# Summing the query-state product of odd chunks in the banks of the score-value product

## The chip, the cores and the metric

One core of one Trainium2 chip runs the whole kernel. The metric is the device time of one execution in microseconds (us), the median of the runs shown.

## The reference

A delta-rule recurrence (four sequences, 8 heads, 768 steps, head size 48), and then a feed-forward layer on its output (3072 tokens, 384 in, 768 hidden).

```python
for t in range(S):
    kt, vt, bt = (k_n[:, :, t], v[:, :, t], beta[:, :, t, None])
    y[:, :, t] = np.einsum('bhd,bhde->bhe', q[:, :, t], state)
    v_old = np.einsum('bhde,bhd->bhe', state, kt)
    state = state + bt[:, :, :, None] * np.einsum('bhd,bhe->bhde', kt, vt - v_old)
...
h = np.maximum(np.maximum(x @ w1, x @ w2), x @ w3)
return (h @ w_out).astype(np.float32)
```

`k_n` is k divided by its norm. x is y with the heads of a token put side by side.

## The kernel before, in words

**Chunks.** The 768 steps are cut into 12 chunks of 64 (`C`). Within a chunk the recurrence is turned into matrix products; only the state `st` (48 x 48 for each sequence and head) goes from chunk to chunk. Two chunks form a group; there are 6 groups (`GROUPS`). The feed-forward layer works on 512 tokens, those of a group, at a time.

**The products of a chunk c.** A chunk has 8 heads and 4 sequences, so 32 small products of each kind, and the array of 128 x 128 is used as four quarters of 64 x 64: the quarter is given by which half of the partitions the operands lie on (row half) and which half the result goes to.
- `old_k` (letter k, lines 750 to 757): keys times state, in `times_state` (line 736, tile p_k, matmuls L743); VectorE subtracts it from the values (L755).
- `old_q` (letter q, lines 759 to 763): queries times state, also in `times_state` (p_q, L743); ScalarE copies it to the tile qs (L763), of which there is one buffer.
- `new` (letter u, L771): the block's triangular inverse times what `old_k` left (p_u); ScalarE copies it to u (L776).
- `step` (letter s, L794): keys times u (p_s); VectorE adds it to the state (L801).
- `to_y` (letter y, L813): masked scores times u (p_y); VectorE adds qs to it (L815), which gives the chunk's y.
- `to_x` (letter x, L832 to L841) turns y into the layer's x on TensorE; from group 2 on `y_blocks`, `read_y` and `turn_y` (letters x, w, X) do it by two transfers and a VectorE transpose (L872).

The inverse comes from a substitution on VectorE (`solve`, L561 and L565) and from products that join its halves (e, f, z and j: `halves_z`, `halves_u` with L696 and its copies L700, `join_z` L713, `join_u` L726). t or T is `turn` (L338, the transposes of keys and queries), g or P is `gram` (L415, scores), M masks scores (L399), and S is one step of `solve`.

**PSUM.** The eight banks are two for the layer (tag "ffn") and three pairs (tag "two", `ps_two`, line 92), one bank for each half of a chunk's sequences. All the products of the recurrence use the pairs. A pair is taken when a product starts and comes free when its reader is done; the pair that has been free longest is taken next. `solve(1)` (group 1) keeps its running sum y_p in a pair from line 524 until its last step (L569).

**Order.** The schedule is written by hand; each engine works in program order. The layer of group m is a generator, `ffn(m)`, whose units (three matmuls of p_h, L1224, or six or more of p_o) are yielded one by one, and after each unit the entries for that step are issued. `FIRST` holds, by step of `ffn(0)`, the recurrence of chunk 1 and the queries that are turned; `EARLY_LINKS` holds group 1 (chunks 2 and 3) in the later steps of `ffn(0)`; `LINKS`, `FOURTH_LINKS` and `LAST_LINKS` hold the later groups. In a name such as "k1", the digit says which chunk of the group. After T4 to T7 `queries` issues the load of a later query block (`load_q`, SyncE's queue). In `ffn(0)` a step also converts a piece of the layer's weights (`weights`: ScalarE L247 to L249, VectorE L259, GpSimd L263).

Of the kernel before, what the change touches and what calls it, by code (L numbers as in the profile page):

```python
# [23 lines left out]
def kernel(  # L24
# [31 lines left out]
    nc = tc.nc  # L56

    B, H, S, D = q.shape
# [5 lines left out]
    NP = H // 2  # L64
# [27 lines left out]
    def ps_two(name):  # L92
        return pairs.tile([128, 2, 512], FP32, name=name, tag="two", bufs=3)
# [24 lines left out]
    def rows(bb):  # L118
        return slice(C * bb, C * (bb + 1))

    def dims(par):
        return slice(DP * par, DP * par + D)
# [77 lines left out]
    st = const.tile([128, 2, 2, NP, D], FP32, name="st")  # L200
# [113 lines left out]
    kqts, ats, pts, xs, at_d = {}, {}, {}, {}, {}  # L314
# [89 lines left out]
    def gram(n, parts=(0, 1), queues=one_queue, copy=nc.scalar.copy, later=False):  # L404
        kqt, g = kqts[n], n % 2
        p_g = ps_two("p_g")

        whole = len(parts) == 2 and not g
        for j in range(NP):
            for par in range(2):  # L410
                for bb in range(2):
                    kq = kqt[dims(par), j, bb ^ g]
                    for i in (0,) if whole else parts:
                        c0 = j * 128 + i * C
                        nc.tensor.matmul(  # L415
                            p_g[
                                rows(bb ^ (g * i)), par, c0 : c0 + C * (1 + whole)
                            ],
                            kq[:, 0],
                            kq if whole else kq[:, i],  # L420
                        )
        p_v = p_g.rearrange("p two (j i t) -> p two j i t", j=NP, i=2)
        if 1 in parts:
            pt = pts[n] = square("pt")
            if later:
                copy(by_par(pt), p_v[:, :, :, 1])
            else:
                masked(pt, p_v[:, :, :, 1])
        if 0 not in parts:
            return  # L430
        at = ats[n] = square("at")
        copy(by_par(at), p_v[:, :, :, 0])  # L432
        if queues:
            to_dram(n, queues)
# [181 lines left out]
    def both(name, w, bufs=1):  # L616
        return work.tile([128, 2, H, w], FP32, name=name, bufs=bufs)

    def by_head(t, w):
        return t[:, :, 0 : H * w].rearrange("p g (h x) -> p g h x", x=w)  # L620
# [3 lines left out]
    def block(bb, f=0, n=BL):  # L624
        return slice(C * bb + BL * f, C * bb + BL * f + n)
# [23 lines left out]
    def heads_of(c, name, w):  # L649


        copies = (nc.scalar.copy,) if c else (nc.scalar.copy, nc.vector.tensor_copy)
        n = H // len(copies)
        for i, copy in enumerate(copies):
            p_v = ps_two(name)[:, :, 0 : n * w]
            yield (
                range(i * n, i * n + n),
                p_v.rearrange("p g (h x) -> p g h x", x=w), copy,
            )
# [13 lines left out]
    def span(hs):  # L673
        return slice(hs[0], hs[-1] + 1)
# [53 lines left out]
                negate[bb](u12[block(bb), :, span(hs)], p_v[bb][block(bb)], -1.0)  # L728


    xts, rhss, qss, us, yts = {}, {}, {}, {}, {}

    def heads(t):
        return t.rearrange("p g (j two) d -> p two (g j) d", two=2)

    def times_state(kqt, i, name):
        p_b = ps_two(name)
        for j in range(NP):
            for g in range(2):
                for par in range(2):  # L740
                    for bb in range(2):
                        c0 = (g * NP + j) * D
                        nc.tensor.matmul(  # L743
                            p_b[rows(bb), par, c0 : c0 + D],
                            kqt[g][dims(par), j, bb ^ g, i],
                            st[dims(par), bb ^ g, g, j],
                        )
        return p_b[:, :, 0 : H * D].rearrange("p two (x d) -> p two x d", d=D)

    def old_k(c):  # L750
        rhss[c] = vts.pop(c)
        if c:
            kqt = [kqts[2 * c + g] for g in range(2)]
            rhs = heads(rhss[c])
            nc.vector.tensor_tensor(  # L755
                out=rhs, in0=rhs, in1=times_state(kqt, 0, "p_k"), op=ALU.subtract
            )

    def old_q(c):
        kqt = [kqts[2 * c + g] for g in range(2)]  # L760
        if c:
            qs = qss[c] = both("qs", D)
            nc.scalar.copy(heads(qs), times_state(kqt, 1, "p_q"))  # L763

    def new(c):
        rhs = rhss.pop(c)
        u = us[c] = both("u", D, 2)
        for hs, p_v, copy in heads_of(c, "p_u", D):
            for i, h in enumerate(hs):
                for bb, g in TILES:  # L770
                    nc.tensor.matmul(  # L771
                        p_v[rows(bb ^ g), g, i],
                        ut[c % NU][rows(bb), g, h],
                        rhs[rows(bb), g, h],
                    )
            copy(u[:, :, span(hs)], p_v)  # L776
        if c + NU < 2 * FINE:
            for bb in range(2):
                corner = ut[c % NU][block(bb), :, :, BL:C]
                zero = kpad[0][block(bb), None, 0:1, D : D + 1]  # L780
                nc.scalar.copy(corner, zero.to_broadcast(corner.shape))
# [23 lines left out]
    def to_y(c):  # L805
        u = us[c]
        pt = [pts.pop(2 * c + g) for g in range(2)]
        y = yts[c] = both("y", D)
        for hs, p_v, copy in heads_of(c, "p_y", D):
            for i, h in enumerate(hs):  # L810
                for bb, g in TILES:
                    r = rows(bb ^ g)
                    nc.tensor.matmul(p_v[rows(bb), g, i], pt[g][r, h], u[r, g, h])  # L813
            if c:
                nc.vector.tensor_tensor(out=y, in0=qss.pop(c), in1=p_v, op=ALU.add)  # L815
            else:
                copy(y[:, :, span(hs)], p_v)
# [536 lines left out]
    for _ in range(2):  # L1354
# [6 lines left out]
    join_u(0)  # L1361
    masked(pts[1], by_par(pts[1]))
    old_k(0)
    old_q(0)
    new(0)
    some(conv, 1)
    fetch(nc.gpsimd)
    load_v(1, nc.gpsimd)
    placed(1, 3)
    to_y(0)  # L1370
    halves_t(1)
    solving = solve(1)
# [6 lines left out]

    LINKS = {  # L1380
# [3 lines left out]
    }  # L1384
    FOURTH_LINKS = {
# [2 lines left out]
    }  # L1388
    LAST_LINKS = {
        0: "k0 q0", 6: "p1", 8: "d0 d1 z0 z1", 9: "j0 j1", 10: "u0", 11: "s0 y0",  # L1390
        12: "x0 k1 q1", 13: "u1 w0", 14: "y1 x1", 15: "w1", 16: "X0", 19: "X1",
    }

    STEPS = {
# [6 lines left out]
    EARLY_LINKS = {  # L1401
# [3 lines left out]
    }  # L1405


    FIRST = {
# [3 lines left out]
    }  # L1412


    RECURS = dict(
        z=join_z, j=join_u, k=old_k, q=old_q, u=new, s=step, y=to_y, x=to_x,
        e=halves_z, f=halves_u, d=turn_t1,
    )
    MADE = dict(V=load_v, P=prep_values)
# [2 lines left out]
        g=lambda n: gram(n, queues=(nc.gpsimd,) * 2 if n in (10, 11) else one_queue),  # L1422
# [132 lines left out]
```

## Time and profile before

| | |
|---|---|
| median of the 3 runs shown | 505.97 us (505.88 to 508.54) |
| span of the profiled execution, first to last instruction | 505.2 us |
| TensorE matmul busy, share of the span | 484.0 us, 96% |
| VectorE busy | 361.1 us, 71% |
| ScalarE busy | 169.4 us, 34% |
| GpSimd busy | 187.1 us, 37% |
| mean granted TensorE clock | 0.968 |

The profiled execution's own time outside the span is not listed; its span lies 0.8 us below the median of the runs. PE is TensorE's matmuls, PEld its weight loads, DVE VectorE, ACT ScalarE, POOL GpSimd, SP SyncE. A matmul of this kernel's 32-bit numbers leaves two records, so 32 matmuls read "x64". An arrow `a<-b` in a tile column reads "a, made from b"; `<-DVE v_t L755` after an idle time names what ended it.

### The profile page before, as it was taken

To read this page: it belongs to the slowest core of one execution; us is meant where nothing else is said; L and a number is where in the kernel's file an instruction comes from. 1 tells how busy PE (TensorE), PEld (TensorE's weight loads), DVE (VectorE), ACT (ScalarE), POOL (GpSimd) and SP (SyncE) were. 2 spreads that over 40 slices of the span, in tenths; PEclk is the share of its full clock that TensorE was granted. 3 is DMA by queue.
4 is the path that set the end of the run, shared out by engine and by line. 5 is a ranking of instruction groups with operands and counts; after the bars stand their busy time and mean duration, and the time that the engine had idled before them with its cause. 6 is when DMAs were issued, how large, how long until landed. Compare 5 with 4: busy or idle time off the path is not lost.

```text
span 505.2 us, 18676 instructions
## 1 busy us (share of the span) xinstructions
PE 484.0 (96%) x8064; PEld 338.0 (67%) x8064; DVE 361.1 (71%) x835; ACT 169.4 (34%) x320; POOL 187.1 (37%) x311
## 2 busy tenths in 40 slices
PE   7678989999999999999999999999999999999996
PEld 6467767855566555565565565555797457998895
DVE  5888799787996441799652999565998874468753
ACT  5585664885422142210152200242201032212210
POOL 7434472793391935770395880501000020000000
PEclk9855899999999999999999999999999999999999
DMA  8937869864045934544584652744224230340002
GB/s 114 205 50 214 195 142 160 198 181 137 3 120 134 191 72 77 146 119 117 112 156 104 158 137 74 149 72 96 64 54 90 47 86 15 85 94 1 0 18 47
DMA packets 109121, 53.50 MB, mean 106 GB/s; under 512 B 92208, under 2 KB 102864, under 8 KB 109040
## 3 DMA queue, kind: packets, MB, share of 16 engines
q1 hardware_dynamic: 97280, 31.78, 31.0%
q0 software_dynamic: 9216, 19.85, 16.5%
q8 instruction: 63, 1.03, 0.9%
q10 hardware_dynamic: 2544, 0.69, 0.8%
q14 instruction: 18, 0.15, 0.1%
HBM read 39.17 MB, written 13.11 MB: 103 GB/s over the span
## 4 chain that ended last, share of the span: by engine, by line
PE 76%; DVE 11%; ACT 4%; DMA 3%; SPq 3%; issue 2%; POOL 0%; DVEq 0%; ACTq 0%; POOLq 0%
PE p_h L1224 28%; PE p_o L985 13%; PE p_o L1262 12%; PE p_c L1163 5%; DVE tmp L561 3%; PE p_g L415 2%; PE p_m L905 2%; PE p_u L771 2%; PE p_k L743 2%; DVE y_p L565 2%; DMA kmore<-in_k_dram 2%; PE p_y L813 2%; PE p_s L794 2%; PE p_q L743 1%; PE p_j L726 1%
## 5 line engine op out<-in xcount | busy, mean ns | idle before, releaser
L1224 PE MATMUL p_h<-xt,w_sb 128*128 128x512 f32 (+1 forms) x450 | 186.8, 558 | 0.6 <-ACT xt L839 0.6
L1224 PEld LDWEIGHTS p_h<-xt,w_sb 128*128 128x128 f32 x450 | 82.4, 193 | 69.2 <-issue 61.6
L1238 DVE TENSOR_TENSOR h<-h,p_h 128x512 f32<-128x512 f32 (+1 forms) x42 | 25.5, 607 | 46.8 <-PE p_h L1224 46.3
L565 DVE TENSOR_TENSOR y_bl<-y_bl,tmp 128x31 f32<-128x31 f32 (+20 forms) x139 | 50.4, 363 | 4.8
L561 DVE TENSOR_TENSOR tmp<-x_bl,y_bl 128x31 f32<-128x31 f32 (+20 forms) x139 | 48.8, 351 | 3.9
L1262 PE MATMUL p_o<-wo_sb,h 128*128 128x384 f32 x144 | 48.9, 490 | 0.0
L373 POOL DMA_DIRECT2D turned<-in_q_dram x72 | 39.3, 554 | 4.6 <-POOL turned L368 3.1
L1262 PEld LDWEIGHTS p_o<-wo_sb,h 128*128 128x128 f32 x144 | 26.7, 190 | 17.2
L1234 ACT ACTIVATE h<-p_h 128x512 f32<-128x512 f32 x24 | 14.3, 597 | 69.2 <-PE p_h L1224 69.2
L263 POOL TENSOR_TENSOR w_sb<-mant,up 128x384 int32<-128x384 int32 x18 | 19.0, 1054 | 39.5 <-DVE mant L259 37.8
L415 PEld LDWEIGHTS p_g<-kqt 48*64 48x64 f32 x1216 | 24.5, 142 | 9.2 <-issue 6.3
L415 PE MATMUL p_g<-kqt 48*64 48x64 f32 (+1 forms) x1216 | 27.7, 241 | 0.9 <-ACT kqt L344 0.8
L1268 ACT COPY o_sb<-p_o 128x384 f32<-128x384 f32 x12 | 5.8, 479 | 62.6 <-PE p_o L1262 56.5
L801 DVE TENSOR_TENSOR st<-st,p_s 48x768 f32<-48x768 f32 (+1 forms) x18 | 17.1, 949 | 12.7 <-PE p_s L794 12.4
L399 DVE TENSOR_TENSOR pt<-p_g,mask 128x512 f32<-128x512 f32 x20 | 13.8, 690 | 17.0 <-PE p_g L415 16.9
L598 POOL DMA_DIRECT2D ut<-y_d x4 | 2.6, 653 | 60.6 <-DMA y_d<-y_bl 60.6
L148 POOL DMA_DIRECT2D v_t<-in_v_dram x14 | 11.6, 832 | 35.3 <-PE p_u L771 35.3
L368 POOL MEMSET turned<- 128x96 f32 x18 | 3.3, 191 | 49.4 <-DVE kqt L389 49.4
L771 PEld LDWEIGHTS p_u<-v_t,ut 64*64 64x64 f32 x768 | 13.5, 141 | 8.4 <-issue 7.3
L432 ACT COPY at<-p_g 128x512 f32<-128x512 f32 x22 | 12.8, 585 | 17.4 <-DVE pt L399 15.4
L373 POOL DMA_DIRECT2D turned<-in_k_dram x32 | 17.5, 556 | 1.2 <-POOL turned L368 1.2
L1163 PE MATMUL p_c<-xt,w_sb 128*128 128x256 f32 x72 | 17.7, 379 | 0.0
(239 smaller groups left out, 907.3 us busy)
## 6 DMA issues: line engine op xcount, KB each, us to landing
w_bits<-in_moe_w_dram SPq DMA_DIRECT2D x9, 384.0 KB, 6.2
w_bits<-in_moe_w_dram POOLq DMA_DIRECT2D x9, 384.0 KB, 5.7
turned<-in_q_dram POOLq DMA_DIRECT2D x72, 48.0 KB, 2.8
out_dram<-o_sb SPq DMA_DIRECT2D x36, 96.0 KB, 2.3
y_x<-y SPq DMA_DIRECT2D x32, 96.0 KB, 3.0
qall<-y_x SPq DMA_DIRECT2D x32, 96.0 KB, 2.8
v_t<-in_v_dram POOLq DMA_DIRECT2D x14, 192.0 KB, 5.0
at_d<-at SPq DMA_DIRECT2D x72, 32.0 KB, 3.0
```

Source lines behind the costliest of these rows:

```text
L263: nc.gpsimd.tensor_tensor(out=dst.bitcast(I32), in0=mant_v.bitcast(I32), in1=up_v, op=ALU.add)
L373: (queue, nc.gpsimd)[i].dma_start(out=t[p0 : p0 + 32, bb, at : at + NP * 2 * D].rearrange("p (j x) -> p j x", j=NP), in_=(k, q)[i][2 * bb ...
L415: nc.tensor.matmul(p_g[rows(bb ^ (g * i)), par, c0 : c0 + C * (1 + whole)], kq[:, 0], kq if whole else kq[:, i],)
L561: nc.vector.tensor_tensor(out=t_v, in0=row.to_broadcast(t_v.shape), in1=column.to_broadcast(t_v.shape), op=ALU.mult,)
L565: nc.vector.tensor_tensor(out=rest, in0=rest, in1=t_v, op=ALU.subtract)
L771: nc.tensor.matmul(p_v[rows(bb ^ g), g, i], ut[c % NU][rows(bb), g, h], rhs[rows(bb), g, h],)
L801: nc.vector.tensor_tensor(out=s_v[r], in0=s_v[r], in1=p_s[r, :, 0 : H * D], op=ALU.add)
L985: nc.tensor.matmul(to[:, g], a[j][:, 128 * g : 128 * (g + 1)], b[j], start=(start and g == j == 0), stop=(stop and g == 1 and j == len(a) ...
L1163: nc.tensor.matmul(to, w[stays], moves, start=(n == 0), stop=(n == len(terms) - 1))
L1224: nc.tensor.matmul(p_h, w_sb[i][:, t, f * 128 : (f + 1) * 128], xt[:, t, lo : lo + w], start=(t == 0), stop=(t == KT - 1),)
L1238: nc.vector.tensor_tensor(out=h, in0=h, in1=p_h, op=ALU.max)
L1262: nc.tensor.matmul(p_o, stays, moves, start=(n == 0), stop=(n == len(terms) - 1))
```

## The change

For odd chunks the query-state product is no longer written to a pair of its own and copied to qs. `old_q` now has two parts of 16 matmuls. Part 0 (letter a) takes the pair p_y and writes half of the heads into it; part 1 writes the other half into the same pair, from inside `new`, after the first half of its heads. In each part a row half of the array writes one bank. Later `to_y` adds the score-value product onto it in PSUM (`start` off), and ScalarE copies the sum to y. The pair is held from part 0 to that copy. Even chunks keep qs and the addition (`even_q`); the call for chunk 0, which did nothing but look up tiles, is gone. In the tables, q of odd chunks is gone, "a1" stands ahead of "k1", and x0 of group 1 moves one step, behind s1.

```diff
-    def old_q(c):
+    def old_q(c, part):
+        if part == 0:
+            sums_y[c] = by_head(ps_two("p_y"), D)
+        for j in range(NP):
+            for g in range(2):
+                par = g ^ part
+                for bb in range(2):
+                    nc.tensor.matmul(
+                        sums_y[c][rows(bb), g, 2 * j + par],
+                        kqts[2 * c + g][dims(par), j, bb ^ g, 1],
+                        st[dims(par), bb ^ g, g, j],
+                        start=(part == 0 and j == 0),
+                        stop=False,
+                    )
+    def even_q(c):
         kqt = [kqts[2 * c + g] for g in range(2)]
-        if c:
-            qs = qss[c] = both("qs", D)
-            nc.scalar.copy(heads(qs), times_state(kqt, 1, "p_q"))
+        qs = qss[c] = both("qs", D)
+        nc.scalar.copy(heads(qs), times_state(kqt, 1, "p_q"))
 
     def new(c):
...
             for i, h in enumerate(hs):
+                if c in sums_y and h == NP:
+                    old_q(c, 1)
                 for bb, g in TILES:
...
     def to_y(c):
...
-        for hs, p_v, copy in heads_of(c, "p_y", D):
+        if c in sums_y:
+            held = [(range(H), sums_y.pop(c), nc.scalar.copy)]
+        else:
+            held = heads_of(c, "p_y", D)
+        for hs, p_v, copy in held:
             for i, h in enumerate(hs):
                 for bb, g in TILES:
                     r = rows(bb ^ g)
-                    nc.tensor.matmul(p_v[rows(bb), g, i], pt[g][r, h], u[r, g, h])
-            if c:
+                    nc.tensor.matmul(
+                        p_v[rows(bb), g, i], pt[g][r, h], u[r, g, h],
+                        start=not c % 2, stop=(not c % 2 or h == H - 1),
+                    )
+            if c in qss:
                 nc.vector.tensor_tensor(out=y, in0=qss.pop(c), in1=p_v, op=ALU.add)
             else:
                 copy(y[:, :, span(hs)], p_v)
...
-    old_q(0)
...
     LINKS = {
...
-        5: "g2 g3 p1", 6: "u0 N0", 7: "V1 N1", 8: "s0 y0 N2", 9: "x0", 10: "k1 q1",
+        5: "g2 g3 p1", 6: "u0 N0", 7: "V1 N1", 8: "s0 y0 N2", 9: "x0", 10: "a1 k1",
...
     LAST_LINKS = {
-        12: "x0 k1 q1", 13: "u1 w0", 14: "y1 x1", 15: "w1", 16: "X0", 19: "X1",
+        12: "x0 a1 k1", 13: "u1 w0", 14: "y1 x1", 15: "w1", 16: "X0", 19: "X1",
...
     EARLY_LINKS = {
-        23: "k1 y0 q1", 24: "u1 x0", 25: "s1", 26: "y1", 28: "x1",
+        23: "a1 k1 y0", 24: "u1", 25: "s1 x0", 26: "y1", 28: "x1",
...
     FIRST = {
-        0: "e1 s0 S1 S1", 1: "f1 k1 S1 S1 S1", 2: "z1 d1 M2 S1 S1",
-        3: "j1 S1 q1 M3 S1 S1", 4: "u1 T4", 5: "y1", 6: "s1 T5", 7: "x1 T6",
+        0: "e1 s0 S1 S1", 1: "f1 a1 k1 S1 S1 S1", 2: "z1 d1 M2 S1 S1",
+        3: "j1 S1 M3 S1 S1", 4: "u1 T4", 5: "y1", 6: "s1 T5", 7: "x1 T6",
...
     RECURS = dict(
-        z=join_z, j=join_u, k=old_k, q=old_q, u=new, s=step, y=to_y, x=to_x,
+        z=join_z, j=join_u, k=old_k, q=even_q, u=new,
+        a=lambda c: old_q(c, 0), s=step, y=to_y, x=to_x,
```

More of the change, by code (lines that the diff above doesn't have):

```diff
@@ L728, in join_u @@
                 negate[bb](u12[block(bb), :, span(hs)], p_v[bb][block(bb)], -1.0)
-    xts, rhss, qss, us, yts = {}, {}, {}, {}, {}
+    xts, rhss, qss, us, yts, sums_y = {}, {}, {}, {}, {}, {}
     def heads(t):
```

## The prediction

> **What bounds the kernel now.** I read the page first (busy shares, slices), then busy time by stage, the waits of TensorE, the chain of waits in order of time, and the timeline of 40 to 136 us.
>
> ```profile
> PE 484.0 (96%) x8064; PEld 338.0 (67%) x8064; DVE 361.1 (71%) x835; ACT 169.4 (34%) x320; POOL 187.1 (37%) x311
> PE   7678989999999999999999999999999999999996
> DVE  5888799787996441799652999565998874468753
> PEclk9855899999999999999999999999999999999999
> ```
>
> TensorE is full from the eighth slice on at full granted clock; VectorE is near full only in the first quarter. By stage (span, then busy time of PE, PEld, DVE, ACT, POOL, the clock, the DMA share, GB/s):
>
> ```profile
> 54.60:81.00 26.40, 24.03 (x664) 19.93 (x658) 23.93 (x59) 17.25 (x34) 13.45 (x17) 1.00 0.84 170
> 81.00:102.00 21.00, 19.98 (x336) 16.49 (x334) 16.93 (x39) 15.59 (x29) 10.97 (x13) 1.00 0.89 176
> 102.00:130.70 28.70, 28.55 (x700) 16.05 (x691) 24.69 (x53) 16.85 (x32) 16.38 (x22) 1.00 0.48 137
> 130.70:242.70 112.00, 112.00 (x1551) 67.08 (x1552) 76.65 (x174) 28.87 (x52) 62.32 (x113) 1.00 0.49 110
> ```
>
> From 130.7 us TensorE has no idle time at all: there, VectorE or ScalarE work that is saved is worth nothing, and only matmul time counts. Chunks 1 and 3 lie before that line or on it, chunks 5, 7, 9 and 11 behind it. TensorE's waits between 44.9 and 131 us, the places where a delay can be swallowed (total, times, longest):
>
> ```profile
> PE p_t L338 <- DMA qall<-in_q_dram: 1.0, 1, 1.0
> PE p_x L832 <- DVE st L801: 0.7, 1, 0.7
> PE p_j L726 <- DVE t L632: 0.3, 1, 0.3
> ```
>
> **The odd chunks behind 130.7 us.** The chain of waits around chunk 9 (start, length, what):
>
> ```profile
> 356.81 1.08 PE p_k L743 x64
> 357.89 0.93 PE p_q L743 x64
> 358.83 2.77 PE p_h L1224 x6
> 361.60 1.08 PE p_u L771 x64
> ```
>
> Each product is 32 matmuls (64 records). One that follows another 64-row product takes 0.93, so 29 ns a matmul; the first after a 128-row matmul takes 0.15 more. The new query product is again 32 matmuls: 16 ahead of p_k and 16 inside p_u. Before: 1.08 + 0.93 + 1.08 = 3.09 us; after: a1 and k1 1.08 + 0.47, p_u 1.08 + 0.47, together 3.10. No change, but for the seams in p_u, where the last quarter of the array that p_u used is the first that the product needs. Bounds: nothing (the chain shows p_k, p_y and p_q at 0.93 each when back to back at 124.7) and, for two seams, two whole matmuls of 0.22 (the mean of p_q's row), 0.44. I take 0.05, near the row of unlike products back to back: 0.25 for chunks 3 to 11.
>
> Do new waits arise here? p_u needs VectorE's subtraction (L755). After the change only the layer's 2.77 us lie between p_k's end and p_u, not 0.93 more. At chunk 9 p_k then ends at 358.36, the subtraction runs as before from 359.07 to 360.02, and p_u starts at 361.1: 1.1 us to spare. At chunk 7 the subtraction ends at 288.07 against 288.5: tight, still free. The three bank pairs go to whoever asks in the order in which they came free; s1 gets the pair that L755 emptied long ago and doesn't wait for the copy of p_y.
>
> ```profile
> L743 PE MATMUL p_q<-st,kqt 48*64 48x48 f32 x672 | 12.2, 218 | 0.0
> L815 DVE TENSOR_TENSOR y<-qs,p_y 128x768 f32<-128x768 f32 x11 | 10.5, 952 | 4.6 <-PE p_y L813 4.4
> L763 ACT COPY qs<-p_q 128x768 f32<-128x768 f32 x11 | 8.8, 800 | 18.1 <-PE p_q L743 11.7 <-DVE y L815 4.7 <-DVE y_p L565 1.7
> ```
>
> Six L815 additions of 0.95 go from VectorE; six L763 copies go and six copies of p_y, same form, 0.80, come: ScalarE's work is unchanged. At chunks 5 to 11 the freed VectorE time is idle time. Cover gone, each would cost its 0.80.
>
> **Chunk 1: one bank pair left.** The second block solve keeps its running sum y_p in one of the three "two" pairs until 89 us. The change holds p_y of chunk 1 in a second pair from step 1 to step 5. So k1, z1, j1, u1 and T4 pass through one pair, each waiting until the one before is read out.
>
> ```profile
> 54.90 1.55 ACT L700 ACTIVATE ut<-p_f 16x256 f32<-16x256 f32 x4 [2.55 <-PE p_f L696]
> 55.91 0.95 DVE L755 TENSOR_TENSOR v_t<-v_t,p_k 128x768 f32<-128x768 f32 x1 [1.61 <-PE p_k L743]
> 66.17 0.80 ACT L776 COPY u<-p_u 128x768 f32<-128x768 f32 x1 [0.63 <-PE p_u L771]
> 70.44 0.95 DVE L815 TENSOR_TENSOR y<-qs,p_y 128x768 f32<-128x768 f32 x1
> ```
>
> Step by step, by these durations:
> - f1 ends at 54.6, a1's 16 matmuls at 55.2. k1 now needs the pair that f1's four copies (L700) read until 56.45: a wait of 1.3. k1 ends at 57.45 (before: 55.8); unit 2, queued behind, and L755, for which VectorE sits idle, slip with it: L755 by 1.64.
> - z1 (needs L755's end, 58.5) starts after unit 2 at 58.95: no more. j1 already waits for VectorE's transposes, which stand behind L755 and slip by the same 1.64. So j1 ends at 62.8 for 61.16.
> - q1's 1.08 behind j1 is gone: unit 4 is late by 0.56. u1 has 0.47 more: 1.04. T4 must wait until L776 has read p_u: 0.1 + 0.80 + 0.05, so unit 5 and y1 are late by 2.0. That is the peak.
> - y1's copy runs on ScalarE at 71.1 to 71.9. Behind it waits conversion 5 (L247 to L249, at 68.92 before), late by 3; POOL needs it only for step 11's weights, six units on.
> - Regained: the L815 at 70.44 is gone, so VectorE, without a gap from 56 to 84 us, is late by 1.64 - 0.95 = 0.69. Before, x1 waited 0.7 for L801 to empty its pair (the second row of the waits); L801 now ends at 74.94, ahead of x1's turn at 75.5. TensorE leaves x1 late by 1.2.
> - T5 and T6 start late, and SyncE issues the query loads behind them late. The load that p_t awaited at 85.84 was issued 10 us earlier, and the next one, 1.8 us younger, landed at 86.2: at a DMA share of 0.84 the backlog, not the issue, sets the landing. I let it land 0 to 1.2 late; so TensorE's lateness there becomes 0.2 to 1.2. The low end is nearer to the two landings.
> - But VectorE ends the solve 0.69 late; stores, reloads and p_z of chunk 3 (from 105.5, its data landing at 105.43) follow. So 0.5 is the floor. I take 0.6.
>
> **Chunk 3** sits on the border:
>
> ```profile
> 130.66 1.02 PEld L771 LDWEIGHTS p_u<-v_t,ut 64*64 64x64 f32 x64 [0.98 <-DVE v_t L755]
> ```
>
> p_u waits for L755, the last of a VectorE queue that is full from 115.7 and is started by ScalarE and TensorE, so it slips by the same 0.6. All 32 matmuls of q1 stood ahead of this wait; now 16 stand in p_u behind it: +0.47, in full, since everything after is solid TensorE. ScalarE's 4.7 us wait in L763 (qs has one buffer, still read by chunk 2's L815) vanishes; TensorE has no wait for ScalarE there: 0.
>
> **Sum:** 0.6 + 0.47 + 0.25 = +1.3 us on the span of 505.2. The median of the three runs shown, 505.97, is 0.8 above that span; launch and end lie around it and don't change. 505.97 + 1.3 = 507.3. The parts' ends give +0.5 + 0.47 = +1.0 and 1.2 + 0.47 + 5 x 0.44 = +3.9.
>
> **Rivals.**
> - *The lateness of chunk 1 stays whole.* If x1 does not regain 0.8 and the query load slips with its issue, 2.0 + 0.47 + 0.25 = +2.7: 508.7. For it: the wait on the single pair is in the code, and DMA is busy. Against it: TensorE had 1.7 us of waits in just these places. It decides once the load of 85.84 lands more than a microsecond later.
> - *The VectorE side gains.* Chunk 3's p_u waits 0.98 because VectorE is behind; two of its operations before that were stretched by POOL's conversions (0.90 for 0.22 at 120.63, 1.06 for 0.28 at 125.77). If the shifted order avoids these 1.4 us, the 0.98 and the 0.47 are paid from it: 0.6 + 0.25 - 0.98 = -0.1, and with chunk 1's lateness fully swallowed about -1: 505.0.
> - *Matmuls of the two row halves that accumulate in one bank take turns.* Now p_y collects products from rows 0 to 63 and from 64 to 127. If only two run at a time where four did, 29 ns become 58: 0.93 for each of chunks 3 to 11, +4.7, and with the sum 512.0. Against it: L813 already sends both halves into each bank of p_y and takes 0.93. The Trainium skill, "TensorEngine Tiling (Array Packing)", section "Restrictions and Gotchas", says that different row tiles cannot use one PSUM bank at the same time. The trace of L813 does not bear this out where the halves write different partitions.
> - *It doesn't do what it says*: the products are the same in number, and the additions do leave; I give this nothing.
>
> **Chances.** A measurement here tells about 0.5% (2.5 us: below 503.4, above 508.5) from no change. Forecast 0.55; lateness whole 0.20 (half of it above 508.5, as its centre is); VectorE gains 0.14 (0.04 below 503.4); row halves 0.06 (above); something unseen 0.05 (0.02 below, 0.03 above). Faster 0.06, same 0.75, slower 0.19. The range leaves out most of the last two and the far part of the gain: 504.6 to 509.9, the top being the parts' upper end.
>
> **What would show it.** Right: a TensorE wait of about 1.3 before k1 (L743) on ScalarE's L700, one of about 0.9 before T4 (L338) on L776; x1 without its wait; p_u at 1.55 in odd chunks, a1 with p_k at 1.55; L815 five times, not eleven. Wrong: p_k of chunk 1 without a wait, p_u above 1.7, new TensorE gaps behind 131 us, or p_u of chunk 3 starting before 130.

## The result and the profile after

The changed kernel takes 510.53 us (median of 10 runs, 508.85 to 511.74), against 506.89 for the kernel before in the same comparison (10 runs, 505.40 to 510.23): ratio 1.0062, interval 1.0039 to 1.0085. Slower, and above the range. Two later comparisons of the same two kernels gave 1.0056 (1.0031 to 1.0081) and 1.0024 (1.0000 to 1.0048). The profiled execution has a span of 508.6 us in a run of 510.28.

The page: the busy times first. VectorE does six operations less; TensorE's matmul count is unchanged.

```profile
PE 485.3 (95%) x8064; PEld 339.1 (67%) x8064; DVE 356.4 (70%) x829; ACT 169.3 (33%) x320; POOL 186.3 (37%) x311
```

By stage, with the window edges moved by 1.6, the difference between the two starts of f1 (p_f, L696: 53.70 before, 55.27 after), so that both tables begin at the same work (span, then busy time of PE, PEld, DVE, ACT, POOL, the clock, the DMA share, GB/s):

```profile
56.20:82.60 26.40, 22.54 (x614) 18.71 (x610) 22.17 (x55) 16.96 (x33) 13.09 (x16) 1.00 0.72 158
82.60:103.60 21.00, 20.73 (x371) 17.18 (x366) 19.09 (x42) 14.81 (x27) 10.19 (x11) 1.00 0.97 183
```

In the first stage TensorE is busy for 22.54 us (24.03 before) and VectorE for 22.17 (23.93 before): both wait more. In the second TensorE catches up on 35 matmul records and VectorE still has 19.09 us of work where it had 16.93. TensorE's longest waits from 44.9 to 140 us (total, times, longest):

```profile
PE p_t L338 <- ACT u L796: 1.7, 1, 1.7
PE p_k L743 <- ACT ut L700: 1.2, 1, 1.2
PE p_u L791 <- DVE v_t L755: 0.9, 1, 0.9
```

The first two are new and stand on the single free bank pair. The timeline of chunk 1 (start, length, engine, what; idle time before it and what ended that):

```profile
56.47 1.54 ACT L700 ACTIVATE ut<-p_f 16x256 f32<-16x256 f32 x4 [2.83 <-PE p_f L696]
58.06 1.15 PE L743 MATMUL p_k<-st,kqt 48*64 48x48 f32 x64 [1.18 <-ACT ut L700]
59.34 0.95 DVE L755 TENSOR_TENSOR v_t<-v_t,p_k 128x768 f32<-128x768 f32 x1 [3.47 <-PE p_k L743]
62.44 0.98 POOL L263 TENSOR_TENSOR w_sb<-mant,up 128x384 int32<-128x384 int32 x1 [5.71 <-DVE mant L259]
...
67.41 0.58 ACT L247 ACTIVATE mant<-w_bits 128x384 f32<-128x384 f32 x1 [0.92 <-POOL w_sb L263]
67.88 0.62 ACT L248 ACTIVATE up<-w_bits 128x384 int16<-128x384 uint32 x1
68.37 0.61 ACT L249 ACTIVATE up<-w_bits 128x384 f16<-128x384 f32 x1
69.01 0.80 ACT L796 COPY u<-p_u 128x768 f32<-128x768 f32 x1
69.86 0.66 PE L338 MATMUL p_t<-ident,qall 128*128 128x128 f32 x4 [1.68 <-ACT u L796]
76.03 0.94 DVE L821 TENSOR_TENSOR st<-st,p_s 128x768 f32<-128x768 f32 x1
91.03 0.20 DVE L565 TENSOR_TENSOR y_p<-y_p,tmp 128x31 f32<-128x31 f32 x1
```

k1 waits for f1's copies, and VectorE sits idle 3.47 us ahead of L755 (1.61 before). From there the delay goes round: VectorE's share of the weight conversion (L259) is late, so POOL's (L263) is, so ScalarE's next one (L247 to L249) stands ahead of the copy of u, and T4 waits for that copy. The last row is the end of the solve.

Chunk 9 in the chain of waits, and chunk 3:

```profile
360.10 0.61 PE p_y L770 x32
360.72 0.93 PE p_k L743 x64
361.65 0.02 issue
361.67 2.84 PE p_h L1251 x6
364.51 0.61 PE p_u L791 x32
365.12 0.47 PE p_y L770 x32
365.59 0.47 PE p_u L791 x32
```

```profile
132.96 0.68 PE L791 MATMUL p_u<-v_t,ut 64*64 64x48 f32 x32 [0.90 <-DVE v_t L755]
```

a1 with k1 takes 1.54 and p_u with the product inside it 1.55, as forecast. The groups show the additions gone and the copies in their place (busy, mean ns | idle time before):

```profile
L842 DVE TENSOR_TENSOR y<-qs,p_y 128x768 f32<-128x768 f32 x5 | 4.8, 954 | 0.1
L844 ACT COPY y<-p_y 128x768 f32<-128x768 f32 x6 | 4.8, 800 | 9.0 <-PE p_y L837 9.0
L781 ACT COPY qs<-p_q 128x768 f32<-128x768 f32 x5 | 4.0, 798 | 7.4 <-PE p_q L743 7.4
```

**How runs are set side by side.** The start of f1 is the last point ahead of every instruction that the change moves. In 16 profiles it lies anywhere from 52.3 to 56.3 us, 53.70, 54.86 and 54.25 with the kernel before, 55.27, 53.64 and 53.94 with the changed one. Spans therefore mislead, and all times below are counted from f1. Three points are enough: the end of the solve (the last L565; after: 91.03 + 0.20 - 55.27 = 35.96), the start of p_u of chunk 3 (132.96 - 55.27 = 77.69), and the end of the span.

| kernel | f1 starts | solve ends | p_u of chunk 3 | end | timed ratio, interval |
|---|---|---|---|---|---|
| before | 53.70 | 34.80 | 76.96 | 451.50 | |
| before_again | 54.86 | 34.78 | 77.28 | 451.80 | 1.0020 (0.9997 to 1.0044) |
| before_third | 54.25 | 34.75 | 78.04 | 452.66 | 0.9982 (0.9956 to 1.0008) |
| after | 55.27 | 35.96 | 77.69 | 453.30 | 1.0062 (1.0039 to 1.0085) |
| after_again | 53.64 | 35.98 | 78.63 | 453.74 | 1.0056 (1.0031 to 1.0081) |
| after_third | 53.94 | 35.95 | 79.21 | 454.38 | 1.0024 (1.0000 to 1.0048) |
| only_chunk_1 | 56.33 | 35.98 | 77.75 | 452.37 | 1.0042 (1.0015 to 1.0069) |
| only_chunk_3 | 53.48 | 34.77 | 76.59 | 451.88 | 1.0015 (0.9992 to 1.0038) |
| only_late | 52.51 | 35.32 | 77.75 | 452.51 | 1.0007 (0.9986 to 1.0029) |
| t4_after_y1 | 56.11 | 35.95 | 78.13 | 453.96 | 1.0035 (1.0012 to 1.0059) |
| q1_ahead_of_k1 | 56.03 | 36.64 | 78.45 | 452.85 | 1.0046 (1.0027 to 1.0065) |
| a1_ahead_of_j1 | 53.02 | 38.40 | 80.35 | 455.56 | 1.0027 (1.0000 to 1.0055) |
| a1_ahead_of_j1_again | 54.51 | 35.59 | 77.39 | 452.60 | 1.0040 (1.0025 to 1.0055) |
| a1_j1_t4_later | 53.32 | 34.09 | 75.87 | 451.28 | 0.9999 (0.9970 to 1.0028) |
| chunk_1_clear | 52.28 | 36.00 | 79.36 | 454.29 | 0.9993 (0.9968 to 1.0018) |
| chunk_1_clear_again | 53.64 | 34.10 | 76.32 | 450.97 | 1.0000 (0.9972 to 1.0027) |

The end of the solve repeats within 0.05 in the three profiles of before and the three of after; it is the sharpest point. From it to p_u of chunk 3 lie 41.7 to 43.4 us in every row: 42.16, 42.50 and 43.29 before, 41.73, 42.65 and 43.26 after. The mean of this stretch is 42.3 in the nine rows whose solve ends at 35.5 or later, and 42.3 in the six whose solve ends at 34.8 or earlier. So a late solve passes on whole, with a chance of its own of 1.6 us on top. From that p_u to the end the six rows of before and after spread by 0.1 (before) and 0.5 (after).

**The clock in four of them.** From f1 to p_u of chunk 3 the granted clock of TensorE is full in twelve of these profiles. In four it falls to 0.50 for a while in chunk 1, each time behind one or more stalls of TensorE: from 62.91 to 66.32 in only_late, from 66.69 to 73.52 in a1_ahead_of_j1, from 67.77 to 71.18 in a1_ahead_of_j1_again and from 66.68 to 70.09 in chunk_1_clear. Two stretches of a1_ahead_of_j1_again, columns as in the stages above (the clock follows POOL's count):

```profile
64.36:67.77 3.41, 1.56 (x84) 1.32 (x76) 3.31 (x8) 2.37 (x4) 0.91 (x2) 1.00 0.33 98
67.77:71.18 3.41, 3.41 (x14) 2.40 (x17) 3.06 (x7) 2.04 (x4) 3.05 (x5) 0.50 0.23 38
```

The solve of these four rows holds what the slow clock cost besides what the edit did.

### The profile page after: what moved, and what is told of

The parts are those of the page before. It is cut to its first block, busy times and chain, and to the rows that moved or that the text cites. A ratio compares the mean times of both kernels' runs of the same rounds, so it can differ in the third digit from the quotient of the medians.

```text
span 508.6 us, 18665 instructions
## 1 busy us (share of the span) xinstructions
PE 485.3 (95%) x8064; PEld 339.1 (67%) x8064; DVE 356.4 (70%) x829; ACT 169.3 (33%) x320; POOL 186.3 (37%) x311
## 4 chain that ended last, share of the span: by engine, by line
PE 81%; DMA 5%; ACT 5%; DVE 4%; issue 2%; SPq 2%; POOL 1%; DVEq 0%; POOLq 0%; ACTq 0%
PE p_h L1251 30%; PE p_o L1012 13%; PE p_o L1289 12%; PE p_c L1190 5%; DMA qall<-in_q_dram 3%; PE p_g L415 3%; PE p_y L837 2%; PE p_u L791 2%; PE p_m L932 2%; PE p_s L814 2%; PE p_k L743 2%; DMA kmore<-in_k_dram 2%; SPq L129 2%; PE p_j L726 1%; PE p_z L713 1%
## 5 line engine op out<-in xcount | busy, mean ns | idle before, releaser
L561 DVE TENSOR_TENSOR tmp<-x_bl,y_bl 128x31 f32<-128x31 f32 (+20 forms) x139 | 50.9, 366 | 3.9
L565 DVE TENSOR_TENSOR y_bl<-y_bl,tmp 128x31 f32<-128x31 f32 (+20 forms) x139 | 48.5, 349 | 4.8
L263 POOL TENSOR_TENSOR w_sb<-mant,up 128x384 int32<-128x384 int32 x18 | 18.8, 1043 | 41.8 <-DVE mant L259 37.2
L755 DVE TENSOR_TENSOR v_t<-v_t,p_k 128x768 f32<-128x768 f32 x11 | 10.4, 949 | 12.9 <-PE p_k L743 12.9
L796 ACT COPY u<-p_u 128x768 f32<-128x768 f32 (+1 forms) x12 | 9.3, 772 | 27.3 <-PE p_u L791 27.2
```

The lines of the kernel that those rows point to most:

```text
L263: nc.gpsimd.tensor_tensor(out=dst.bitcast(I32), in0=mant_v.bitcast(I32), in1=up_v, op=ALU.add)
L561: nc.vector.tensor_tensor(out=t_v, in0=row.to_broadcast(t_v.shape), in1=column.to_broadcast(t_v.shape), op=ALU.mult,)
L565: nc.vector.tensor_tensor(out=rest, in0=rest, in1=t_v, op=ALU.subtract)
```

## The experiments

The theory after the first comparison: the loss is made in chunk 1, by the two waits on the single bank pair, and reaches chunk 3 through VectorE; chunk 3 adds its half product. Rivals: the start of the program changed, the late chunks' seams cost more, or it is TensorE's wait before T4 that is carried on and not VectorE's lateness.

**Both kernels again, first time.** No edit.

> The kernel before, unchanged, as a second profile. In the first two profiles the changed kernel was already 1.6 us late when chunk 1's f1 (p_f, L696) began at 55.3 us instead of 53.7, ahead of the first reordered instruction; from there to the end it took 453.3 us instead of 451.5. Theory (chance): the start-up differs from execution to execution whatever the kernel, so f1 begins somewhere between 53 and 56, and f1 to the end is 451.5 within 0.5; ratio 1.000 within 0.003. Rival (the start-up belongs to the program): f1 begins at 53.7 within 0.3 again.

> The changed kernel, unchanged, as a second profile. Chance: f1 begins anywhere between 53 and 56, f1 to the end is 453.3 within 0.5, so the change itself costs 1.8 us, ratio about 1.004. Rival (start-up belongs to the program): f1 begins at 55.3 within 0.3 again, ratio about 1.006 or more.

The changed kernel repeats its waits (1.19 for k1, 1.69 for T4) and its solve to 0.02, while its f1 starts 1.6 earlier. The start is chance and not the change's: the part of the first pair's difference of spans (508.6 against 505.2) that lies ahead of f1 is not its doing.

**One part of the change at a time.** Each adds a tuple of chunks that are summed and keeps the old order for the others:

```diff
+    SUMMED = (1,)              # only_chunk_1
+    SUMMED = (5, 7, 9, 11)     # only_late
+    SUMMED = (3,)              # only_chunk_3
...
-        a=lambda c: old_q(c, 0), s=step, y=to_y, x=to_x,
+        a=lambda c: old_q(c, 0) if c in SUMMED else None, s=step, y=to_y, x=to_x,
```

> Only chunk 1 sums its query product in the pair of p_y (the table FIRST of the change); chunks 3 to 11 go through qs as before. Theory (one bank pair left): waits of about 1.2 us before k1 on L700 and 1.7 before T4 on L776 as in the changed kernel; after the query load at 86 to 88 us 0.5 to 1.0 us late against the kernel before, counted from f1; f1 to the end 452.0 to 452.5; no 0.5 more at chunk 3. Rival (the accumulation itself is slow wherever it is used): the same small share as any of the six chunks, f1 to the end about 451.8.

> Only chunks 5, 7, 9 and 11 sum in the pair; chunks 1 and 3 as before. Theory: TensorE has no gap there and p_k with half the product takes 1.58 and p_u 1.55, so 0.04 us for each of four chunks: f1 to the end 451.7, ratio 1.000 within 0.003. Rival (matmuls of both row halves into one bank, or the accumulation, cost time): 0.3 us or more for each, f1 to the end 452.7 or more.

> Only chunk 3 is summed in the banks; chunk 1 and chunks 5 to 11 are as before. All numbers count from the start of f1 (the p_f group L696 near 55 us), so that the start of the program, which moves from execution to execution, is out. The theory (half of the query product stands behind p_u's wait for L755, and the rest is chunk 1's): p_u of chunk 3 starts at 77.0 to 77.3 after f1, as in the two profiles of before; from p_u of chunk 3 to p_k of chunk 4 takes 30.84 (30.36 before); from f1 to the end takes 452.1 (451.5 and 451.8 before); ratio about 1.001. Rival one (chunk 3's half is hidden by the wait): 30.36, and 451.65 to the end. Rival two (chunk 3 alone makes the whole loss): 453 or more.

Chunk 1 alone has both waits (1.19 and 1.69) and the late solve, 35.98: the whole lateness is its own. The late chunks alone time at 1.0007, and chunk 3 alone at 1.0015; neither can be told from no change. The profile of only_late lost 1.27 us in a stall of TensorE in j1 of chunk 1, where its code is that of before, and ran at half clock for the 3.41 us that followed; more on such stalls below. What chunk 3 costs is read from p_u of chunk 3 to p_k of chunk 4: 30.36, 30.36 and 30.38 in the three profiles of before, 30.84, 30.82 and 30.83 in those of after, 30.83 in only_chunk_3, 30.37 in only_chunk_1. That is +0.46, in full.

**T4 behind y1.**

```diff
-        3: "j1 S1 M3 S1 S1", 4: "u1 T4", 5: "y1", 6: "s1 T5", 7: "x1 T6",
+        3: "j1 S1 M3 S1 S1", 4: "u1", 5: "y1 T4", 6: "s1 T5", 7: "x1 T6",
```

> All odd chunks as in the change, but T4 (four transposes) moves from step 4 behind y1 in step 5, so that a layer unit lies between u1 and the next product that wants the pair or the copy of u. The theory that T4's wait of 1.7 for the late copy of u is what TensorE carries on: the wait falls to 0.3 or less (now before y1), x1 starts at 20.6 to 20.9 after f1 (21.92 in the change), p_u of chunk 3 at 77.2 or earlier (77.7 and 78.6), and f1 to the end takes 452.3 to 452.6 (453.3 and 453.7). The rival, that it is VectorE's lateness behind L755 (1.6 less the addition saved) that reaches chunk 3: x1 starts earlier all the same, but p_u of chunk 3 stays at 77.7 or later and the end at 453.3 or later, with a longer wait at the query load or at chunk 3's p_u.

T4's 1.7 is gone (0.22 is left ahead of y1, 0.28 ahead of s1), and it buys nothing: the solve ends at 35.95, x1 starts at 21.76 after f1 (21.92 in the change). The waits of TensorE show who took it back:

```profile
PE p_k L744 <- ACT ut L700: 1.2, 1, 1.2
PE p_x L861 <- DVE st L822: 0.8, 1, 0.8
```

x1 again waits for VectorE (L822 is L801 of before). The rival is right here: VectorE's lateness is enough by itself.

**a1 ahead of j1, and T4 behind y1.** p_y of chunk 1 is held two steps less, so k1 finds a free pair.

```diff
-        0: "e1 s0 S1 S1", 1: "f1 a1 k1 S1 S1 S1", 2: "z1 d1 M2 S1 S1",
-        3: "j1 S1 M3 S1 S1", 4: "u1 T4", 5: "y1", 6: "s1 T5", 7: "x1 T6",
+        0: "e1 s0 S1 S1", 1: "f1 k1 S1 S1 S1", 2: "z1 d1 M2 S1 S1",
+        3: "a1 j1 S1 M3 S1 S1", 4: "u1", 5: "y1 T4", 6: "s1 T5", 7: "x1 T6",
```

> As the run with T4 behind y1, and a1 moves from step 1 to step 3, ahead of j1: p_y of chunk 1 is held two steps less, and k1 finds a free pair as before. Both theories of chunk 1 then have nothing left to carry: no wait of k1 for L700, L755 of chunk 1 on time, no wait of T4. Expected by the theory (waits on the single pair cost 1.2, chunk 3's half 0.47, the seams the rest): p_u of chunk 3 at 76.9 to 77.3 after f1, f1 to the end 452.0 to 452.4, ratio 1.001. The rival (the later loss is not the pair's but the summed order's own, a1 in two parts): 453 or more.

With neither wait the whole loss of chunk 1 goes and turns round: the solve ends 0.7 earlier than before, at 34.09, p_u of chunk 3 starts at 75.87, and the ratio is 0.9999. All the odd chunks are still summed.

**Only one of the two waits.** Two ways to have k1's or T4's alone. With a1 ahead of j1 and T4 left in step 4, only T4 waits:

> All odd chunks as in the change, and a1 moves from step 1 to step 3, ahead of j1; T4 stays in step 4 behind u1. So k1's wait for L700 is gone and T4's wait for the copy of u is not. Theory (VectorE's lateness, which begins at k1, is the whole loss of chunk 1): L755 of chunk 1 ends 3.16 after the start of f1, as before (5.03 in the change); VectorE's last subtraction of the solve (L565) ends by 34.8 (36.0 in the change, 34.8 before, 34.1 with T4 moved too); T4 still waits, for 0.9, the 0.80 copy and a little, since that copy now starts on time; p_u of chunk 3 starts at 75.9 to 76.9 and f1 to the end takes 451.3 to 451.9. Rival (T4's wait counts too): x1 starts at 21.0 or later, p_u of chunk 3 at 77.5 or later, the end at 452.8 or more.

This profile decided nothing: TensorE stalled three times in work that waited for nothing shown, 0.58, 0.97 and 1.75, and its clock was 0.50 for 6.83 us. The same kernel again:

> The run with a1 ahead of j1 and T4 in its place, again: its profile had three stalls of TensorE in which it waited for nothing shown (0.58, 0.97 and 1.75 at matmul records 1105, 1232 and 1359), after a start of f1 at 53.0. With f1 at 53.3 or later only the last is to be expected, of about 1. Theory (k1's wait, by way of VectorE, is the whole loss of chunk 1): solve ends at 34.1 to 34.8, p_u of chunk 3 at 75.9 to 77.4, f1 to the end 451.3 to 452.3. Rival (T4's wait of 0.9 counts by itself): solve at 35.0 or later, f1 to the end 452.6 or more. If the stalls come again with a later f1, they belong to this order.

```profile
66.23 0.45 PE L792 MATMUL p_u<-v_t,ut 64*64 64x48 f32 x17 [0.93 <-issue]
67.60 1.00 PE L338 MATMUL p_t<-ident,qall 128*128 128x128 f32 x4 [0.92 <-ACT u L797]
68.39 2.77 PE L1253 MATMUL p_h<-xt,w_sb 128*128 128x256 f32 x6
71.09 1.17 PE L839 MATMUL p_y<-u,pt 64*64 64x48 f32 x64
73.68 1.15 PE L815 MATMUL p_s<-u,kpad 64*64 64x48 f32 x64
74.90 0.95 DVE L822 TENSOR_TENSOR st<-st,p_s 128x768 f32<-128x768 f32 x1 [1.30 <-PE p_s L815]
```

L755 ends at 3.16, as before, and yet the solve ends 0.8 later than before and 1.5 later than with neither wait. These are the rival's numbers, but T4's wait is not shown to be their cause. A stall of 0.93 lies ahead of the wait of 0.92, and behind both the clock is 0.50. T4 takes 1.00 and the six matmuls behind it 2.77, where the run with neither wait, at full clock, has 0.66 and 1.46:

```profile
67.98 0.66 PE L338 MATMUL p_t<-ident,qall 128*128 128x128 f32 x4
68.47 1.46 PE L1253 MATMUL p_h<-xt,w_sb 128*128 128x256 f32 x6
```

Up to L822 VectorE is only 0.09 behind that run; there it stands idle 1.30 us for p_s. From the start of T4 to that of y1 TensorE takes 3.49 (67.60 to 71.09), where the change takes 1.88 at full clock (69.86 to 71.74): 1.61 more. An estimate from these rows: 1.61 earlier, p_s would have ended before VectorE was ready for it, and T4's wait would have cost the solve next to nothing. So the theory that k1's wait is the whole loss of chunk 1 missed its numbers here and is not refuted.

The two timed ratios of this order, 1.0027 and 1.0040, lie above the 0.9999 with neither wait. The clock fell in both of its profiles; whether T4's wait makes it fall, and how often in the timed runs, is not shown. A stall of 0.91 without T4's wait, in a1_j1_t4_later, left it at 1.00. With all odd chunks summed, the solve ends at 34.09 with neither wait, 35.95 with k1's alone, 35.96 with both, and 35.59 with T4's alone and the slow clock.

The other way is the kernel of before with q1 moved ahead of k1: nothing is summed, no pair is held, and only k1 waits.

```diff
-        0: "e1 s0 S1 S1", 1: "f1 k1 S1 S1 S1", 2: "z1 d1 M2 S1 S1",
-        3: "j1 S1 q1 M3 S1 S1", 4: "u1 T4", 5: "y1", 6: "s1 T5", 7: "x1 T6",
+        0: "e1 s0 S1 S1", 1: "f1 q1 k1 S1 S1 S1", 2: "z1 d1 M2 S1 S1",
+        3: "j1 S1 M3 S1 S1", 4: "u1 T4", 5: "y1", 6: "s1 T5", 7: "x1 T6",
```

> The kernel of before (no product is summed in the banks, all additions stay) with one move: q1 of chunk 1 goes from step 3 to step 1, ahead of k1, so that q1 takes the free pair and k1 waits for L700 as in the change. No pair is held, and T4 has nothing to wait for. Theory (k1's wait alone makes VectorE late, and VectorE's lateness passes whole to chunk 3): L755 of chunk 1 ends 5.0 after the start of f1 (3.16 before), VectorE's solve, with no addition saved, ends 1.9 to 2.1 late at 36.7 to 36.9, p_u of chunk 3 starts at 78.9 to 80.1 (mean of before 77.4), f1 to the end takes 453.6 to 454.5, ratio 1.004. Rival (the waits behind the solve swallow it; it is the held pair and T4 that cost): solve late, but f1 to the end 452.5 or less, ratio 1.001 or less.

```profile
58.84 1.15 PE L743 MATMUL p_k<-st,kqt 48*64 48x48 f32 x64 [0.72 <-ACT ut L700]
60.11 0.95 DVE L755 TENSOR_TENSOR v_t<-v_t,p_k 128x768 f32<-128x768 f32 x1 [3.48 <-PE p_k L743]
```

L755 ends at 5.03, exactly as in the change, and the solve at 36.64, 1.86 late. The end, 452.85, is between the two theories' numbers: only 41.81 us lay between solve and p_u this time, the low end of that chance. The ratio, 1.0046, is what the theory expected. So one reordered product, with no summing at all, costs in the timing what the change costs, and k1's wait is enough for it.

**Only chunk 1 summed, without the waits.** The one addition that VectorE is spared where it is full, and nothing else of the change.

> Only chunk 1 is summed, with a1 ahead of j1 and T4 behind y1; chunks 3 to 11 as before. This keeps the addition that VectorE is spared (0.95, in the stretch where it is full) without the waits. If VectorE's time ahead of 131 us counts: p_u of chunk 3 up to 0.9 earlier than before (76.1 to 76.9 after f1 for 77.0 to 77.3), f1 to the end 450.7 to 451.4 for 451.5 and 451.8. If loads and stores set chunk 3's start instead: 451.5 to 451.8, no change. If the pair held by chunk 1 costs something even so: above 452.

> The run with only chunk 1 summed and a1 and T4 moved, again: its profile had two stalls of TensorE (1.23 and 1.48) in which it waited for nothing shown, at the 1231st and the 1359th matmul record, after the earliest start of f1 of all (52.3). If these belong to an early start and not to the kernel: with f1 at 53.3 or later there is no stall at record 1231, p_u of chunk 3 starts 75.9 to 76.9 after f1, and f1 to the end takes 450.7 to 451.3; timed ratio 0.997 to 1.000. If they belong to the kernel, both stalls come again and the end takes 454.

The first profile met two stalls, with the half clock behind the second of them. The second profile met one stall at full clock, and came out as expected (34.10, 76.32, 450.97: 1.0 less than the mean of before, 451.99). Timed, the two comparisons give 0.9993 and 1.0000: no gain that these intervals can show. No version here is shown to beat the kernel before.

**Both kernels, third time.** No edit.

> The kernel of before, for a third profile. From f1 to the end 451.5 to 451.8, VectorE's solve ends at 34.8 after f1, a stall of about 1 at matmul record 1359; ratio 1.000. If the two profiles of before were lucky ones: 452.5 or more.

> The changed kernel, for a third profile. From f1 to the end 453.3 to 453.7, VectorE's solve ends at 36.0 after f1, no stall at record 1359, waits of 1.2 (k1) and 1.7 (T4); ratio 1.004 to 1.006. If the loss shown in two profiles were chance, one near 452 is to be expected.

Solve, waits and the stall of before came as expected; the ends were 0.9 and 0.7 above the expected numbers, by the chance between solve and p_u. The means of three are 451.99 before and 453.81 after.

## Why the prediction was wrong

By the means of three profiles each, the change costs, from f1 on: 1.19 to the end of the solve, -0.10 from there to p_u of chunk 3 (a stretch that moves by 1.6 on its own), 0.74 from there to the end; together 1.8. The lowest end of after, 453.30, lies above the highest of before, 452.66. The forecast had 1.3.

- **Chunk 1, forecast 0.6, measured 1.1.** This is the mis-sized term: "VectorE ... is late by 1.64 - 0.95 = 0.69". L755 came 1.87 late, not 1.64, because a product that starts after a wait takes 1.15 (58.06) and I had used the 0.93 of one that follows another. And the addition that was spared gave back 0.69 and not 0.95: in the two undisturbed profiles without waits (34.09 and 34.10) the solve ends 0.69 earlier. 1.87 - 0.69 = 1.18, the measured lateness. The other 0.26: the operation behind the addition started 0.09 before the addition's end (71.30 against 70.44 + 0.95), and that operation, L259, takes 0.56 where the addition is gone and 0.39 before. Why L259 is longer is not shown.
- **"So 0.5 is the floor. I take 0.6."** That VectorE's lateness, not TensorE's, is what chunk 3 gets was right; that some of it gets lost on the way was not. Behind the solve everything follows it.
- **T4's wait, forecast 0.95, measured 1.68.** I took the copy of u to start when p_u ends. ScalarE had three conversion operations ahead of it (67.41 to 68.98), late by way of POOL and VectorE. I had followed that chain only for what it does six units later. In the change the wait is masked, since VectorE is late by as much: without it (t4_after_y1) the solve ends at 35.95 all the same. What it costs alone stays open, since the clock was at half in both profiles that have it alone.
- **TensorE's lateness at x1, forecast 1.2, measured 1.3** (21.92 against 20.58). Two errors cancelled: T4's wait was longer, and TensorE of before had one more loss here, which the view of waits listed and I left out: 1.01, 0.90 and 0.74 in p_u of chunk 1 in its three profiles. None of the three profiles of after has it.
- **Chunk 3, forecast 0.47, measured 0.46.** Right, and so were p_u and a1 with k1 at 1.55.
- **The seams, forecast 0.25, not resolved.** From p_k of chunk 4 to the start of p_c, 54.4 ahead of the end, lie 289.79 before and 290.06 after, means of three, so 0.27. But the three of after run from 289.88 to 290.36, and only_chunk_3, which sums nothing in this stretch, has 290.05. From the rows shown, chunk 9 takes 5.95 from a1 to the end of p_u (360.10 to 366.05) against 5.87 from k1 (356.81 to 362.68), 0.08 more.
- **"The two row halves take turns"** was ruled out: L770's 16 matmuls, with one row half in each bank, take 0.47, or 29 ns each. p_y (L837) of chunk 9, accumulating onto them from both row halves, takes 1.08 in the chain of waits, as it did before (L813); less the 0.15 that the first product behind a 128-row matmul takes more, that is 29 ns each as well. The Trainium skill, "TensorEngine Tiling (Array Packing)", section "Restrictions and Gotchas", says that different row tiles cannot use one PSUM bank at the same time; no doubling shows in these durations.
- **The base.** The median of three runs, 505.97, was low: 506.89 (10 runs), 507.21 (31), 507.34 (35), 508.04 (35) and 507.77 (21) followed for the same kernel. I also took 0.8 us to lie around the span, by setting a median against another execution's span. Where a profiled run's own time is known, 1.7 lies around it (510.28 - 508.6); by that the profiled execution of before took 506.9, and 506.9 + 1.3 would have been 508.2.

Of the 3.2 us between 507.3 and 510.53, 0.9 is the base (506.89 against 505.97) and 0.5 the size. The remaining 1.8 is the first comparison's difference (3.6) beyond what the profiles show (1.8). The mean of the three ratios is 1.0047, or 2.4 us; 1.8, a ratio of 1.0036, lies in the second and third interval and just below the first. I leave the last half microsecond open.

Of the rivals, "the lateness of chunk 1 stays whole" has the title of what happened, and its 2.7 lies nearer to the 2.4 of the timing than the forecast's 1.3 does; to the 1.8 of the profiles the forecast lies nearer. Its mechanism was another one: it needed x1 not to regain its wait and the query load to land late. x1 lost its wait as forecast, and the load's wait was 0.27, 0.38 and 0.8 in the three profiles of after, against 1.01, 0.17 and 0.90 before. What stays whole is VectorE's lateness, by way of the solve.

## What to carry to other kernels

Two engines that hand work to each other in a short loop are late together. Taking away TensorE's longer wait bought nothing, because VectorE was late from the shorter one ahead of it, and that one alone cost as much as both. Only the order without either showed what the change itself was worth, which was nothing that could be measured. Before a change holds a buffer longer, list who takes the next one: here p_k had to wait, and what stood behind p_k on another engine set the price. Compare profiles from the last point ahead of the change, look at the granted clock of the stretch before a wait is given the blame for a delay, and base a forecast on more than three runs where runs differ by 1%.

## What was not expected of the hardware

**Stalls at fixed places of the instruction stream.** TensorE stops now and then with nothing shown to wait for. In all the profiles with such a loss in chunk 1 it falls on matmul record 1358 or 1359, counted from 0 (p_u), or, 128 records earlier, on 1231 to 1233 (p_j or p_z), twice also on 1105 (0.58 in a1_ahead_of_j1, 0.25 in only_late). From the chain of chunk_1_clear (start, length):

```profile
59.44 1.23 issue
60.67 0.57 PE p_j L726 x39
61.23 1.49 PE p_h L1253 x6
62.73 0.61 PE p_u L792 x32
63.34 0.47 PE p_y L771 x32
63.81 0.23 PE p_u L792 x15
64.03 1.48 issue
65.51 0.45 PE p_u L792 x17
```

The trace has a DMA queue of the kind "instruction" that moves blocks of 16 KB. In the page of after:

```profile
q8 instruction: 63, 1.03, 0.9%
```

That is 63 packets of 16 KB during the run. In chunk_1_clear two of them land at 59.21 and 64.05; TensorE goes on at 60.67 and 65.51, 1.46 after each. In before the packet lands at 64.38 and TensorE goes on at 65.65. Over all 14 such losses at records 1231 to 1233, 1358 and 1359, TensorE goes on 1.27 to 1.58 after a packet has landed. The counts fit too: TensorE has 8064 matmul and 8064 weight load records, which over 63 packets is 256 for each, or 128 matmul records with their weight loads, the distance between two of these places. So it looks as if TensorE had used up its instructions; no experiment changed the packets, and this stays an inference.

I had expected the loss at record 1231 to come with an early start of f1 only (52.3, 52.5 and 53.0 have it, none between 53.3 and 55.3); q1_ahead_of_k1 has it at 56.0 too (0.70), so that is at most half the rule. What it means for reading: none of the three profiles of after has this loss, so k1's wait of 1.18 seems to have taken its place, and two profiles of one kernel can differ by such losses.

**Half the clock behind some of them.** The four falls of the clock listed above last 3.41 us, one 6.83, and each begins within 1.7 us of the end of a stall at one of these records. In chunk_1_clear VectorE waits 1.82 us for p_s behind it, and the solve ends 1.9 later than the second time, when there was the later stall alone and the clock stayed full. Most profiles with a stall kept the full clock, so a stall by itself does not decide it; what does is not shown.
